# Logits of a sliding-window mixer: two bursts of 64 small matmuls in place of four of 32

## The chip, the cores and the metric

The kernel runs on one core of a Trainium2 chip. The metric is the device time of one execution, in microseconds. Three runs of the kernel before gave 169.6, 169.63 and 169.82 us; the median is 169.63.

A core has five engines, each with an instruction stream of its own that runs in order: TensorE (PE, with PEld for its weight loads), VectorE (DVE), ScalarE (ACT), GpSimd (POOL) and SyncE (SP). Here SP issues nearly all transfers from memory, ScalarE issues the small ones that spread the attention weights, and GpSimd does a few fills at the start. Engines wait for one another through semaphores.

## The reference

x is 2048 x 512. Two mixers read it, and a gate blends them row by row:

- g = sigmoid(sum over d of x * gate_w), one number for each row.
- a: q, k, v = x @ wqkv in 32 heads of 16. Row s attends to the eight rows s, s-2, ..., s-14 of its own head (rows before 0 are masked). The logits are q.k / 4, a softmax runs over the eight, the weighted sum of v follows, then @ wo.
- b: layer norm of each row of x, then a token MLP over the 2048 rows: u = gelu(h^T @ w1 + b1) with 1792 hidden units, y = u @ w2 + b2, transposed back.
- out = g * a + (1 - g) * b.

## The kernel before, in words

**The main stream.** TensorE runs one long sequence of 128x128 by 512 matmuls, in four parts: the projections q, k, v (line 594, named pf_ and pj_), the first MLP product (line 790, ph2_ft_qt: hidden tile ft of 14, quarter qt of the 16 row tiles), the second MLP product (line 840, ph3) and the output projection (line 856, wo_i). A block is four such matmuls. ScalarE copies the results out of four PSUM banks: projections at lines 602 and 605, gelu (gel_ft) at 811, the MLP's result (t1_i) at 907.

**The logits.** Projection columns are permuted so that each of four values dl holds four of a head's sixteen elements. VectorE multiplies q by k shifted by 0, 2, 4, 6 rows (wh = 0) or 8 to 14 rows (wh = 1), for each dl: that is f_qkm, line 664, named qkm_wh_dl_c. For wh = 0 each product is made in two halves of the rows (128x4096), for wh = 1 whole (128x8192). The products lie in four buffers PBL: 0 and 1 in region PBUF, 2 and 3 in region ATX. TensorE then sums each product over the 16 elements with small matmuls against a 0/1 matrix RP (f_qkr, line 672), 32 output columns wide, four of them side by side in the array. Each of four PSUM banks (4 to 7) holds the logits of one shift; all four dl accumulate in it. Before the change a stretch ("burst") covers two values of dl and has 32 matmuls: dl 0 and 1 in one operation, dl 2 and 3 in four operations, one for each bank. So there are four bursts, two for each wh. ScalarE copies each finished bank into ATT (lev_wh_wl, line 706).

**The softmax.** VectorE masks the first rows (msk_wh, line 716), takes maxima (sm_ma, sm_mb: line 722, scratch MX in region OUTS), subtracts (736), sums, divides and scales (751, 755); ScalarE does the exponentials (741). The weights go to ATX by transfers on ScalarE's queue (d_atx_u_a), and VectorE forms the weighted sum of v in eight units (avm, ava, avb, avc: lines 775 to 780).

**Statistics and gates.** VectorE computes the layer norm's statistics of the 16 row tiles (ln1_t, line 549), finishes them eight at a time (ln2a to ln2d, then ln_rstd and ln_nmr, called lnr here), and ScalarE normalises x in place (ln3_t, line 573). t_b (line 515) transposes the biases. The gate's sums gz_t (line 648) read a second copy of x: tiles 0 to 11 from XA (region WQKV, loaded by d_xa) and 12 to 15 from XB (loaded by d_xb). In the kernel before XB lies in buffer 2's region.

**The end.** cmb_i (line 877) on VectorE combines wo_i's PSUM bank with t1_i; the last four tiles are done in halves (a, b). Each result is stored at once.

**What sets the order.** No instruction stream is written out by hand. Every operation is given an engine, an estimated duration and the names that it reads and writes (`A(engine, fn, duration, reads, writes, ...)`); a list planner (`_Sched._pass`) walks them through time and puts each at the earliest start on its engine, ties going to the longer remaining path. A burst has a high priority and a `delay` of 0.05 beside a 0.06 latency, so it goes to the first block boundary of the main stream after its planned readiness. The planned order is then fixed, and the chip runs it with semaphores whatever the true durations are. `chain([...])` adds orders by hand: the long one for VectorE (line 936), one for SP (line 945) and one for ScalarE (line 951).

```
A("pe", f_qkr(prs), 2.0, reads=rd, writes=LGA, name="qkr_%d_%d" % (wh, dl), prio=-100, delay=BURST_DELAY)
rt = max(rt, d.end + lat + s_.delay)
```

Of the kernel before, what the change touches and what calls it, by code (L numbers as in the profile page):

```python
# [5 lines left out]
BF16 = mybir.dt.bfloat16  # L6
# [3 lines left out]
AF = mybir.ActivationFunctionType  # L10
# [3 lines left out]
D = 512  # L14
NH = 32
DH = 16
NW = 8
# [6 lines left out]
HC = 256  # L24
NEG = -1.0e9
NOELIDE = False
BURST_DELAY = 0.05
# [306 lines left out]
def bass_gated_mix__sliding_local_dilated__mixer_token_mlp__prompt_kernel(nc, A_x, A_wqkv, A_wo, B_x, B_w1, B_b1, B_w2, B_b2, gate_w, out, dbg=None):  # L334
    with contextlib.ExitStack() as es:
        block = es.enter_context(nc.Block())
        view, pview, off, total = _views(nc, es)
        ps = es.enter_context(nc.psum_tensor("ps", [128, 8, 512], FP32))
        esem = {e: es.enter_context(nc.semaphore("sem_" + e)) for e in ("pool", "act", "dve", "pe")}
        sch = _Sched()  # L340

        x2d = A_x[0]
        xv = x2d.rearrange("(t p) d -> p t d", p=128)
# [23 lines left out]
        ATX = view("ATX", BF16, [(NW * HC, 8), (HC, NW), (1, HC)])  # L367
        ATT = view("ATT", BF16, [(NW * HC, 2), (HC, NW), (1, HC)])
# [47 lines left out]
        A = sch.add  # L416
# [12 lines left out]
        def mk_dma(dst, src):  # L429
            return lambda e: e.dma_start(dst, src)  # L430
# [59 lines left out]
        def ld_w1(j):  # L490
# [4 lines left out]
            if j < 4:  # L495
# [8 lines left out]
                       writes=["wo"], deps=throttle(), after=prev_dma(), name="d_wo")  # L504
# [4 lines left out]
        for i_, (v_, n_) in enumerate(((B_b1, NFT), (B_b2, NST))):  # L509
            vr = v_.rearrange("(t q j) -> q t j", q=4, j=32)  # L510
            for q_ in range(4):
                sch.dma("sp", mk_dma(psub(BR, 32 * q_, n_, 32 * i_, [(1, 32)]), vr[q_]), n_ * 64, ds_b, reads=["br"],
                        writes=["br_%d_%d" % (i_, q_)], deps=throttle(), after=prev_dma(), name="d_b_%d_%d" % (i_, q_), issue=0.45)
        d_w1.append(ld_w1(3))
        A("dve", lambda e: e.transpose(out=BT, in_=BR), 0.2, reads=["br_%d_%d" % (i_, q_) for i_ in range(2) for q_ in range(4)],
          writes=["btc"], name="t_b")
# [29 lines left out]
        for hf in range(2):  # L546
            t0 = 8 * hf
            for t in range(t0, t0 + 8):
                A("dve", (lambda t_: (lambda e: e.bn_stats(out=ST6[:, t_, :], in_=X[:, t_, :])))(t), 0.59,  # L549
                  reads=["x%d" % t], writes=["st6_%d" % t], name="ln1_%d" % t, prio=0)  # L550
# [13 lines left out]
              reads=["zc%d" % hf], writes=["sd%d" % hf], name="ln_sqrt%d" % hf, prio=0)  # L564
            A("dve", (lambda t0_: (lambda e: e.reciprocal(out=cols(RSTD, t0_, 8), in_=cols(SD, t0_, 8))))(t0), 0.25,
              reads=["sd%d" % hf], writes=["rstd%d" % hf], name="ln_rstd%d" % hf, prio=0)
# [43 lines left out]
        for (b0, d0, d1, s0, s1) in ((0, 0, 1, 0, 512), (0, 1, 2, 0, 512), (0, 2, 3, 0, 512), (0, 3, 4, 0, 512), (4, 0, 2, 0, 512), (4, 2, 4, 0, 512)):  # L610
            for b in range(b0, b0 + 4):
                tn, dl = first[b]
# [21 lines left out]

        GWB = view("XT", BF16, [(1, D)], extra=NFT * D)
        XA = view("WQKV", BF16, [(D, 12), (1, D)])
        XB = view("ATX", BF16, [(D, 4), (1, D)], extra=3 * NW * HC)
        ds_xb = sch.dsem("xb")
        sch.dma("sp", mk_dma(XB, xv[:, 12:16, :]), 4 * 128 * D * 2, ds_xb, writes=["xb"], name="d_xb")
        ds_gw = sch.dsem("gw")  # L640
        gsrc = bass.AP(gate_w.tensor, gate_w.offset, [[0, 128], [1, D]])
        sch.dma("sp", mk_dma(GWB, gsrc), 128 * D * 2, ds_gw, writes=["gwb"], deps=[last_main[0]], name="d_gw")
# [3 lines left out]
        for t in range(NST):  # L646
            src = XA[:, t, :] if t < 12 else XB[:, t - 12, :]
            A("dve", (lambda s_, t_: (lambda e: e.scalar_tensor_tensor(out=s_, in0=s_, scalar=1.0, in1=GWB, op0=ALU.mult, op1=ALU.mult,  # L648
                                                                       accum_out=col(GZ, t_))))(src, t),
              0.6, reads=["xa" if t < 12 else "xb", "gwb"], writes=["gz%d" % t], name="gz_%d" % t)  # L650
        A("act", lambda e: e.activation(out=TH, in_=GZ, func=AF.Tanh, scale=0.5), 0.25, reads=["gz%d" % t for t in range(NST)],
          writes=["th"], name="g_tanh", prio=0)
        A("dve", lambda e: e.tensor_scalar(out=G, in0=TH, scalar1=0.5, scalar2=0.5, op0=ALU.mult, op1=ALU.add), 0.15,
# [12 lines left out]
        def f_qkr(pairs, wls=(0, 1, 2, 3)):  # L666
            def fn(e):
                ins = None
                for wl in wls:
                    for (dl, buf) in pairs:  # L670
                        for c in range(4):
                            ins = e.matmul(ps[32 * c:32 * c + 32, 4 + wl, :], lhsT=RP, rhs=PBL[buf][:, wl, c * 512:(c + 1) * 512],  # L672
                                           start=(dl == 0), stop=(dl == 3), tile_position=(0, 32 * c))
                return ins
            return fn

        def pbn(buf):
            return ["pb%d_0" % buf, "pb%d_1" % buf] if buf < 3 else ["lb0", "lb1"]

        LGA = ["lg%d_%d" % (b_, h) for b_ in range(4, 8) for h in range(2)]  # L680
        pb_readers = []
        k_all = ["k5_%d_%d" % (dl, sb) for dl in range(4) for sb in range(4)] + ["k5pad"]
        for wh in range(2):
            if wh == 0:
                pieces = [(dl, 2 * h, 2) for h in range(2) for dl in range(4)]
                bufs = [0, 1, 3, 2]
            else:
                pieces = [(dl, 0, 4) for dl in range(4)]
                bufs = [0, 1, 3, 0]
            for (dl, c0, nc_) in pieces:  # L690
                buf = bufs[dl]
                wr = pbn(buf) if nc_ == 4 else [pbn(buf)[c0 // 2]]
                A("dve", f_qkm(wh, dl, buf, c0, nc_), 4.4 if nc_ == 4 else 2.28,
                  reads=["q5_%d_%d" % (dl, sb) for sb in range(c0, c0 + nc_)] +
                        ["k5_%d_%d" % (dl, sb) for sb in range(max(c0 - 1, 0), c0 + nc_)] + ["k5pad"],
                  writes=wr, name="qkm_%d_%d_%d" % (wh, dl, c0), prio=0)
                if c0 + nc_ == 4 and dl % 2 == 1:
                    prs = [(dl - 1, bufs[dl - 1]), (dl, bufs[dl])]
                    rd = sum([pbn(b_) for _, b_ in prs], []) + ["rp"]
                    if dl == 1:  # L700
                        A("pe", f_qkr(prs), 2.0, reads=rd, writes=LGA, name="qkr_%d_%d" % (wh, dl), prio=-100, delay=BURST_DELAY)
                    else:
                        for wl in range(4):
                            qop = A("pe", f_qkr(prs, (wl,)), 0.5, reads=rd, writes=["lg%d_0" % (4 + wl), "lg%d_1" % (4 + wl)],
                                    name="qkr_%d_%d_%d" % (wh, dl, wl), prio=-100 + wl, delay=BURST_DELAY)
                            A("act", (lambda wh_, wl_: (lambda e: e.activation(out=ATT[:, :, 4 * wh_ + wl_, :], in_=ps[:, 4 + wl_, :].rearrange("p (h c) -> p h c", h=2), func=AF.Copy)))(wh, wl),
                              0.55, reads=["lg%d_0" % (4 + wl), "lg%d_1" % (4 + wl)], writes=["lw%d" % (4 * wh + wl)],
                              name="lev_%d_%d" % (wh, wl), prio=0)
                        pb_readers.append(qop)
            def f_msk(wh_):  # L710
                def fn(e):
                    res = []
                    for w in range(4 * wh_, 4 * wh_ + 4):
                        if w == 0:
                            continue
                        res.append(e.memset(psub(ATT, 0, 32, w * HC, [(1, 2 * w)]), NEG))
                    return res
                return fn
            A("dve", f_msk(wh), 0.3, writes=["lw%d" % w for w in range(4 * wh, 4 * wh + 4)], name="msk_%d" % wh, prio=0)
# [41 lines left out]
        for u in range(8):  # L761
            c, hf = u // 2, u % 2
# [57 lines left out]
        def ld_w2(j2):  # L820
            ds = sch.dsem("w2_%d" % j2)
            al = []
            dp = []
            if j2 < 2:
                dp = [byq["qkr_1_1"]]
            elif j2 == 2:
                al = ["wqkv%d_%d" % (tn, dt) for tn in range(3) for dt in range(4)] + ["gz%d" % t for t in range(12)]
            return sch.dma("sp", mk_dma(W2S[j2 % 3], w2v[:, :, 256 * j2:256 * j2 + 256]), F * 256 * 2, ds,
                           writes=["w2s%d" % (j2 % 3)] + al, deps=dp, name="d_w2_%d" % j2)
# [90 lines left out]
        def chain(names):  # L920
            for a_, b_ in zip(names, names[1:]):
                byname[b_].order.add(byname[a_])

        def ln1(*ts):
            return ["ln1_%d" % t for t in ts]

        def ln2(hf):
            return ["ln2%s%d" % (c_, hf) for c_ in "abcd"]

        def gz(*ts):  # L930
            return ["gz_%d" % t for t in ts]

        def lnr(hf):
            return ["ln_rstd%d" % hf, "ln_nmr%d" % hf]

        chain(["rp"] + ln1(0, 1, 2, 3) + ["qkm_0_0_0", "qkm_0_1_0"] + ln1(4, 5, 6, 7) + ln2(0)
              + ["qkm_0_2_0"] + lnr(0) + ["qkm_0_3_0", "qkm_0_0_2"] + ln1(8, 9) + ["qkm_0_1_2"] + ln1(10, 11, 12) + ["qkm_0_2_2"] + ln1(13, 14)
              + ["qkm_0_3_2", "qkm_1_0_0"] + ln1(15) + ln2(1) + ["t_b", "qkm_1_1_0"] + lnr(1)
              + ["qkm_1_2_0", "msk_0", "sm_ma0", "sm_mb0", "qkm_1_3_0"] + gz(12, 13, 14, 15, 0, 1) + [
                 "msk_1", "sm_ma1", "sm_mb1", "sm_m1", "sm_sub0", "sm_sub1"]  # L940
              + ["%s%d" % (n_, h_) for h_ in range(2) for n_ in ("sm_sa", "sm_sb", "sm_s1", "sm_rcp", "sm_nrm")] + gz(*range(2, 12))
              + ["%s_%d" % (n_, u) for k_ in range(4) for n_ in ("avm", "ava", "avb", "avc") for u in USEQ[2 * k_:2 * k_ + 2]] + ["cmb_%d" % i for i in range(HT0)] + ["cmb_%d%s" % (i, x_) for i in range(HT0, NST) for x_ in "ab"])
        byname["d_xb"].deps.update(byname["qkr_0_3_%d" % w] for w in range(4))
        byname["d_w1_6"].deps.add(byname["d_atx_2_3"])
        chain(["d_xb", "d_gw", "d_xa", "d_w2_0", "d_w2_1", "d_w1_4", "d_w1_5", "d_w1_6", "d_w2_2"])
        def atn(u):
            return ["d_atx_%d_%d" % (u, a_) for a_ in range(4)]

# [99 lines left out]
```

## Time and profile before

| | us |
|---|---|
| median of three runs | 169.63 |
| the profiled execution, its own time | 169.63 |
| span of the profiled execution | 167.8 |
| TensorE busy | 162.4 |
| VectorE busy | 150.7 |
| ScalarE busy | 75.0 |

The granted TensorE clock is full speed in every slice. "Busy" counts overlapped instructions once; the matmuls are pipelined, so their own durations (379 ns) are longer than the distance between two of them. The page's part 4 follows back, from the last instruction, what released each step. The timelines quoted below give, for each row, its start and its length in us from the span's start, the engine, line, operation, operands with shapes, the number of instructions merged into the row, and in brackets the idle time before it with what ended it.

### The profile page before, as it was taken

What the parts mean: (1) busy time and instruction counts of PE and PEld (TensorE: products, weight loads), DVE (VectorE), ACT (ScalarE), POOL (GpSimd) and SP (SyncE); (2) the same over time, 40 slices, a digit from 0 to 9 for tenths busy, and PEclk for the clock granted to TensorE, in tenths of its full rate; (3) what the DMA queues carried; (4) which work ended last, traced back from release to release, by engine and by line L of the source; (5) the groups of instructions that cost most, each with busy time, mean ns of one, the idle gap of its engine ahead of it and who ended that gap; (6) DMA issues with size and microseconds to landing.
All of it is one profiled execution on the core that took longest, in us unless ns stands there. A gap on an engine that the chain in (4) does not pass through costs nothing.

```text
span 167.8 us, 2139 instructions
## 1 busy us (share of the span) xinstructions
PE 162.4 (97%) x843; PEld 77.3 (46%) x858; DVE 150.7 (90%) x153; ACT 75.0 (45%) x115; POOL 0.7 (0%) x8
## 2 busy tenths in 40 slices
PE   7899999999999999999999999999999999999993
PEld 3455555544454444444444444444444444444462
DVE  0038999999999997799999999999999999999995
ACT  3087698898979819781131221131321312210000
POOL 1000000000000000000000000000000000000000
PEclk9999999999999999999999999999999999999999
DMA  6999999966304999555799906472573370000554
GB/s 145 286 244 273 280 325 292 298 190 174 129 0 115 356 294 287 152 145 145 177 276 328 288 9 151 103 207 83 147 219 116 103 223 0 0 0 0 184 181 139
DMA packets 47610, 29.64 MB, mean 177 GB/s; under 512 B 9841, under 2 KB 46449, under 8 KB 47601
## 3 DMA queue, kind: packets, MB, share of 16 engines
q1 hardware_dynamic: 45776, 25.11, 54.2%
q10 hardware_dynamic: 1824, 4.39, 9.4%
q8 instruction: 7, 0.11, 0.3%
q14 instruction: 3, 0.02, 0.0%
HBM read 21.11 MB, written 2.10 MB: 138 GB/s over the span
## 4 chain that ended last, share of the span: by engine, by line
PE 93%; DMA 3%; DVE 2%; issue 1%
PE ps L840 29%; PE ps L790 29%; PE ps L594 25%; PE ps L856 6%; PE ps L672 4%; DMA arena<-in_A_x_dram 3%; DVE arena L877 2%
## 5 line engine op out<-in xcount | busy, mean ns | idle before, releaser
L790 PE MATMUL ps<-arena 128*128 128x512 bf16 x219 | 48.2, 379 | 0.5 <-issue 0.3
L840 PE MATMUL ps<-arena 128*128 128x512 bf16 x220 | 48.5, 379 | 0.2
L594 PE MATMUL ps<-arena 128*128 128x512 bf16 x188 | 41.4, 379 | 1.1 <-DMA arena<-in_A_x_dram 0.7
L664 DVE TENSOR_TENSOR arena<-arena 128x4096 bf16<-128x4096 bf16 (+1 forms) x12 | 35.7, 2992 | 0.8 <-ACT arena L605 0.8
L775 DVE TENSOR_TENSOR arena<-arena 128x8192 bf16<-128x8192 bf16 x8 | 35.0, 4418 | 0.0
L790 PEld LDWEIGHTS ps<-arena 128*128 128x128 bf16 x224 | 21.7, 98 | 26.8 <-issue 0.8
L840 PEld LDWEIGHTS ps<-arena 128*128 128x128 bf16 x224 | 21.9, 98 | 26.4
L594 PEld LDWEIGHTS ps<-arena 128*128 128x128 bf16 x192 | 21.5, 113 | 21.0 <-issue 1.1
L907 ACT ACTIVATE arena<-ps,arena 128x512 bf16<-128x512 f32 x16 | 12.5, 778 | 39.4 <-PE ps L840 35.6
L778 DVE TENSOR_TENSOR arena<-arena 128x4096 bf16<-128x4096 bf16 (+1 forms) x16 | 27.0, 1752 | 0.0
L605 ACT ACTIVATE arena<-ps 128x512 bf16<-128x512 f32 x32 | 18.6, 597 | 5.3 <-PE ps L594 5.1
L811 ACT ACTIVATE arena<-ps,arena 128x512 bf16<-128x512 f32 x14 | 9.6, 689 | 23.7 <-PE ps L790 20.8
L549 DVE BATCH_NORM_STATS2 arena<-arena 128x6 f32<-128x512 bf16 x16 | 10.2, 682 | 9.8 <-DMA arena<-in_A_x_dram 9.8
L856 PE MATMUL ps<-arena 128*128 128x512 bf16 (+1 forms) x78 | 14.1, 335 | 0.1
L602 ACT ACTIVATE arena<-ps 128x512 bf16<-128x512 f32 x16 | 9.0, 597 | 7.4 <-PE ps L594 7.3
L573 ACT ACTIVATE arena<-arena 128x512 bf16<-128x512 bf16 x16 | 12.0, 803 | 0.0
L877 DVE SCALAR_TENSOR_TENSOR arena<-ps,arena 128x512 bf16<-128x512 f32 (+1 forms) x20 | 11.5, 638 | 0.4 <-PE ps L856 0.2
L856 PEld LDWEIGHTS ps<-arena 128*128 128x128 bf16 x80 | 7.8, 98 | 6.2
L648 DVE SCALAR_TENSOR_TENSOR arena<-arena 128x512 bf16<-128x512 bf16 x16 | 9.9, 686 | 0.0
L722 DVE TENSOR_TENSOR arena<-arena 128x512 bf16<-128x512 bf16 (+4 forms) x11 | 7.3, 667 | 1.2 <-ACT arena L741 0.8
L672 PE MATMUL ps<-arena 128*32 128x512 bf16 x128 | 7.6, 380 | 0.0
L780 DVE TENSOR_TENSOR arena<-arena 128x1024 bf16<-128x1024 bf16 x8 | 5.5, 689 | 0.1
(38 smaller groups left out, 37.6 us busy)
## 6 DMA issues: line engine op xcount, KB each, us to landing
arena<-in_B_w_dram SPq DMA_DIRECT2D x7, 1024.0 KB, 8.6
arena<-in_B_w_dram SPq DMA_DIRECT2D x8, 896.0 KB, 5.2
arena<-arena ACTq DMA_DIRECT2D x32, 128.0 KB, 2.7
arena<-in_A_x_dram SPq DMA_DIRECT2D x4, 512.0 KB, 4.7
out_dram<-arena SPq DMA_DIRECT2D x15, 128.0 KB, 1.7
arena<-in_A_x_dram SPq DMA_DIRECT2D x1, 1536.0 KB, 8.4
arena<-in_A_wqkv_dram SPq DMA_DIRECT2D x2, 256.0 KB, 3.9
arena<-in_A_x_dram SPq DMA_DIRECT2D x2, 256.0 KB, 3.9
```

What stands on the lines that cost most here:

```text
L573: A("act", (lambda t_: (lambda e: e.activation(out=X[:, t_, :], in_=X[:, t_, :], func=AF.Identity, scale=col(RSTD, t_), bias=col(NMR, t_)) ...
L594: ins = e.matmul(ps[:, bank, s0:s1], lhsT=lhsT, rhs=XT[:, dt, sb * 512 + s0:sb * 512 + s1], start=(dt == 0 and s0 == 0), stop=(dt == 3))
L605: return lambda e: e.activation(out=dst, in_=ps[:, bank, :], func=AF.Copy)
L664: return lambda e: e.tensor_tensor(out=PBL[buf][:, :, 512 * c0:512 * (c0 + nc_)], in0=in0, in1=in1, op=ALU.mult)
L672: ins = e.matmul(ps[32 * c:32 * c + 32, 4 + wl, :], lhsT=RP, rhs=PBL[buf][:, wl, c * 512:(c + 1) * 512], start=(dl == 0), stop=(dl == 3), ...
L775: A("dve", (lambda o_, i0, i1: (lambda e: e.tensor_tensor(out=o_, in0=i0, in1=i1, op=ALU.mult)))(pv, in0, in1), 4.4, reads=v_res + ["atx_% ...
L778: A("dve", (lambda pv_, n__: (lambda e: e.tensor_tensor(out=pv_[:, 0:n__], in0=pv_[:, 0:n__], in1=pv_[:, n__:2 * n__], op=ALU.add)))(pv, n ...
L790: ins = e.matmul(ps[:, bank, :], lhsT=W1W[:, slot, st, 128 * e_:128 * e_ + 128], rhs=X[:, st, :], start=(st == 0), stop=(st == NST - 1))
L840: ins = e.matmul(ps[:, bank, :], lhsT=W2S[slot][:, ft, 128 * e_:128 * e_ + 128], rhs=UT[:, ft, :], start=(ft == 0), stop=(ft == NFT - 1))
L856: ins = e.matmul(ps[:, bank, 0:c1 - c0], lhsT=OT[:, t, 128 * i:128 * i + 128], rhs=WO[:, t, c0:c1], start=(t == 0), stop=(t == 3))
L877: A("dve", (lambda i_, b_, c0_, c1_: (lambda e: e.scalar_tensor_tensor(out=T1[:, i_, c0_:c1_], in0=ps[:, b_, 0:c1_ - c0_], scalar=col(G, i ...
L907: A("act", (lambda i_, bank_: (lambda e: e.activation(out=T1[:, i_, :], in_=ps[:, bank_, :], func=AF.Identity, scale=col(OMG, i_), bias=co ...
```

## The change

- A burst covers all four dl: 64 matmuls, in four operations of 16, one for each PSUM bank, charged 0.92 each by the planner. There are two bursts, one for each wh, each ready when all its products are.
- For wh = 1 the four products take four different buffers (0, 1, 3, 2), where dl = 3 used buffer 0 a second time.
- XB moves from buffer 2's region to OUTS, which the maxima use as scratch: the gates 12 to 15 are declared as writers there, and they now stand ahead of msk_0, sm_ma0 and sm_mb0 on VectorE. d_xb no longer waits for the first half's logits.
- In VectorE's order ln1_10 to ln1_15 with ln2 stand behind the last product of wh = 0, not among them; lnr(1) stands a product earlier; msk_0 with its maxima stands behind qkm_1_3.
- On SP d_xb goes behind d_w1_3, and d_w1_4 goes ahead of d_w2_0 and d_w2_1. These two load into buffer 1's region and now wait for the second burst.

The core of the diff:

```diff
-        XB = view("ATX", BF16, [(D, 4), (1, D)], extra=3 * NW * HC)
+        XB = view("OUTS", BF16, [(D, 4), (1, D)])
...
-                bufs = [0, 1, 3, 0]
+                bufs = [0, 1, 3, 2]
...
-                if c0 + nc_ == 4 and dl % 2 == 1:
-                    prs = [(dl - 1, bufs[dl - 1]), (dl, bufs[dl])]
-                    rd = sum([pbn(b_) for _, b_ in prs], []) + ["rp"]
-                    if dl == 1:
-                        A("pe", f_qkr(prs), 2.0, reads=rd, writes=LGA, name="qkr_%d_%d" % (wh, dl), prio=-100, delay=BURST_DELAY)
-                    else:
-                        for wl in range(4):
-                            qop = A("pe", f_qkr(prs, (wl,)), 0.5, reads=rd, writes=["lg%d_0" % (4 + wl), "lg%d_1" % (4 + wl)],
-                                    name="qkr_%d_%d_%d" % (wh, dl, wl), prio=-100 + wl, delay=BURST_DELAY)
...
+            rd = sum([pbn(b_) for b_ in bufs], []) + PBX[wh] + ["rp"]
+            for wl in range(4):
+                qop = A("pe", f_qkr(list(enumerate(bufs)), (wl,)), 0.92, reads=rd, writes=["lg%d_0" % (4 + wl), "lg%d_1" % (4 + wl)],
+                        name="qkr_%d_%d" % (wh, wl), prio=-100 + wl, delay=BURST_DELAY)
...
-                dp = [byq["qkr_1_1"]]
+                dp = [byq["qkr_1_3"]]
...
-              + ["qkm_0_2_0"] + lnr(0) + ["qkm_0_3_0", "qkm_0_0_2"] + ln1(8, 9) + ["qkm_0_1_2"] + ln1(10, 11, 12) + ["qkm_0_2_2"] + ln1(13, 14)
-              + ["qkm_0_3_2", "qkm_1_0_0"] + ln1(15) + ln2(1) + ["t_b", "qkm_1_1_0"] + lnr(1)
-              + ["qkm_1_2_0", "msk_0", "sm_ma0", "sm_mb0", "qkm_1_3_0"] + gz(12, 13, 14, 15, 0, 1) + [
+              + ["qkm_0_2_0"] + lnr(0) + ["qkm_0_3_0", "qkm_0_0_2"] + ln1(8, 9) + ["qkm_0_1_2", "qkm_0_2_2", "qkm_0_3_2"] + ln1(*range(10, 16)) + ln2(1)
+              + ["t_b", "qkm_1_0_0"] + lnr(1) + ["qkm_1_1_0"]
+              + ["qkm_1_2_0", "qkm_1_3_0"] + gz(12, 13, 14, 15) + ["msk_0", "sm_ma0", "sm_mb0"] + gz(0, 1) + [
...
-        byname["d_xb"].deps.update(byname["qkr_0_3_%d" % w] for w in range(4))
...
-        chain(["d_xb", "d_gw", "d_xa", "d_w2_0", "d_w2_1", "d_w1_4", "d_w1_5", "d_w1_6", "d_w2_2"])
+        chain(["d_w1_3", "d_xb", "d_gw", "d_xa", "d_w1_4", "d_w2_0", "d_w2_1", "d_w1_5", "d_w1_6", "d_w2_2"])
```

More of the change, by code (lines that the diff above doesn't have):

```diff
@@ L636, in bass_gated_mix__sliding_local_dilated__mixer_token_mlp__prompt_kernel @@
         XA = view("WQKV", BF16, [(D, 12), (1, D)])
-        XB = view("ATX", BF16, [(D, 4), (1, D)], extra=3 * NW * HC)
+        XB = view("OUTS", BF16, [(D, 4), (1, D)])
         ds_xb = sch.dsem("xb")
-        sch.dma("sp", mk_dma(XB, xv[:, 12:16, :]), 4 * 128 * D * 2, ds_xb, writes=["xb"], name="d_xb")
+        sch.dma("sp", mk_dma(XB, xv[:, 12:16, :]), 4 * 128 * D * 2, ds_xb, writes=["xb"] + ["outs%d" % k for k in range(4)], name="d_xb")
         ds_gw = sch.dsem("gw")
@@ L649, in bass_gated_mix__sliding_local_dilated__mixer_token_mlp__prompt_kernel @@
                                                                        accum_out=col(GZ, t_))))(src, t),
-              0.6, reads=["xa" if t < 12 else "xb", "gwb"], writes=["gz%d" % t], name="gz_%d" % t)
+              0.6, reads=["gwb"] + (["xa"] if t < 12 else ["xb"]), writes=["gz%d" % t] + ([] if t < 12 else ["outs%d" % (t - 12)]), name="gz_%d" % t)
         A("act", lambda e: e.activation(out=TH, in_=GZ, func=AF.Tanh, scale=0.5), 0.25, reads=["gz%d" % t for t in range(NST)],
@@ L681, in bass_gated_mix__sliding_local_dilated__mixer_token_mlp__prompt_kernel @@
         pb_readers = []
+        PBX = [[], []]
         k_all = ["k5_%d_%d" % (dl, sb) for dl in range(4) for sb in range(4)] + ["k5pad"]
@@ L696, in bass_gated_mix__sliding_local_dilated__mixer_token_mlp__prompt_kernel @@
                   writes=wr, name="qkm_%d_%d_%d" % (wh, dl, c0), prio=0)
-                if c0 + nc_ == 4 and dl % 2 == 1:
-                    prs = [(dl - 1, bufs[dl - 1]), (dl, bufs[dl])]
-                    rd = sum([pbn(b_) for _, b_ in prs], []) + ["rp"]
-                    if dl == 1:
-                        A("pe", f_qkr(prs), 2.0, reads=rd, writes=LGA, name="qkr_%d_%d" % (wh, dl), prio=-100, delay=BURST_DELAY)
-                    else:
-                        for wl in range(4):
-                            qop = A("pe", f_qkr(prs, (wl,)), 0.5, reads=rd, writes=["lg%d_0" % (4 + wl), "lg%d_1" % (4 + wl)],
-                                    name="qkr_%d_%d_%d" % (wh, dl, wl), prio=-100 + wl, delay=BURST_DELAY)
[L706 to L709, printed above, removed]
+            rd = sum([pbn(b_) for b_ in bufs], []) + PBX[wh] + ["rp"]
+            for wl in range(4):
+                qop = A("pe", f_qkr(list(enumerate(bufs)), (wl,)), 0.92, reads=rd, writes=["lg%d_0" % (4 + wl), "lg%d_1" % (4 + wl)],
+                        name="qkr_%d_%d" % (wh, wl), prio=-100 + wl, delay=BURST_DELAY)
+                A("act", (lambda wh_, wl_: (lambda e: e.activation(out=ATT[:, :, 4 * wh_ + wl_, :], in_=ps[:, 4 + wl_, :].rearrange("p (h c) -> p h c", h=2), func=AF.Copy)))(wh, wl),
+                  0.55, reads=["lg%d_0" % (4 + wl), "lg%d_1" % (4 + wl)], writes=["lw%d" % (4 * wh + wl)],
+                  name="lev_%d_%d" % (wh, wl), prio=0)
+            pb_readers.append(qop)
             def f_msk(wh_):
```

## The prediction

> **What bounds the kernel now.** First the page: its busy line and its chain.
>
> ```profile
> PE 162.4 (97%) x843; PEld 77.3 (46%) x858; DVE 150.7 (90%) x153; ACT 75.0 (45%) x115; POOL 0.7 (0%) x8
> PE 93%; DMA 3%; DVE 2%; issue 1%
> PE ps L840 29%; PE ps L790 29%; PE ps L594 25%; PE ps L856 6%; PE ps L672 4%; DMA arena<-in_A_x_dram 3%; DVE arena L877 2%
> ```
>
> TensorE is busy for 97% of the span and carries 93% of the chain, so what it saves counts, if VectorE, 90% busy, can follow. Next, the TensorE timeline (start, us, engine, line, operation, count): L672 is the logits' bursts, and between them lies the main stream.
>
> ```profile
> 33.81 1.91 PE L672 MATMUL ps<-arena 128*32 128x512 bf16 x32
> 35.89 5.13 PE L594 MATMUL ps<-arena 128*128 128x512 bf16 x23 [0.17 <-issue]
> 40.95 1.91 PE L672 MATMUL ps<-arena 128*32 128x512 bf16 x32
> 43.03 7.72 PE L594 MATMUL ps<-arena 128*128 128x512 bf16 x35 [0.17 <-issue]
> 50.59 1.03 PE L790 MATMUL ps<-arena 128*128 128x512 bf16 x4
> 51.55 1.91 PE L672 MATMUL ps<-arena 128*32 128x512 bf16 x32
> 53.62 8.58 PE L790 MATMUL ps<-arena 128*128 128x512 bf16 x39 [0.16 <-issue]
> 62.13 1.91 PE L672 MATMUL ps<-arena 128*32 128x512 bf16 x32
> 64.19 38.80 PE L790 MATMUL ps<-arena 128*128 128x512 bf16 x176 [0.16 <-issue]
> 102.83 45.49 PE L840 MATMUL ps<-arena 128*128 128x512 bf16 x206
> ```
>
> No waits on VectorE stand here: each burst finds its products ready. Three narrow windows of the timeline show a burst inside (the first, second and last group).
>
> ```profile
> 33.81 0.40 PE L672 MATMUL ps<-arena 128*32 128x512 bf16 x4
> 34.03 0.39 PE L672 MATMUL ps<-arena 128*32 128x512 bf16 x4
> ...
> 35.33 0.39 PE L672 MATMUL ps<-arena 128*32 128x512 bf16 x4
> ```
>
> From burst to burst are 7.14, 10.60 and 10.58 us, and by the code six, ten and ten blocks of four main matmuls lie between (a record is missing after each burst, so I count in the code). Four blocks more thus take 3.46 and 3.44 us: 0.863 a block on the mean, 0.216 a matmul. A burst takes the rest, 7.14 - 6 x 0.863 = 1.96, and 1.97 and 1.95 in the other intervals. Inside it four small matmuls start together, and the eight groups are (35.33 - 33.81) / 7 = 0.217 apart. Eight groups are 1.73; so each burst costs 0.23 at its borders, whatever it computes.
>
> Last, the end. VectorE's timeline of the combining line L877, and five of its instructions from narrow windows:
>
> ```profile
> 153.85 3.38 DVE L877 SCALAR_TENSOR_TENSOR arena<-ps,arena 128x512 bf16<-128x512 f32 x5
> 157.42 8.30 DVE L877 SCALAR_TENSOR_TENSOR arena<-ps,arena 128x512 bf16<-128x512 f32 x15 [0.19 <-PE ps L856]
> ```
> ```profile
> 161.74 0.75 DVE L877 SCALAR_TENSOR_TENSOR arena<-ps,arena 128x512 bf16<-128x512 f32 x1
> 162.41 0.48 DVE L877 SCALAR_TENSOR_TENSOR arena<-ps,arena 128x256 bf16<-128x256 f32 x1
> ...
> 164.36 0.48 DVE L877 SCALAR_TENSOR_TENSOR arena<-ps,arena 128x256 bf16<-128x256 f32 x1
> 164.79 0.48 DVE L877 SCALAR_TENSOR_TENSOR arena<-ps,arena 128x256 bf16<-128x256 f32 x1
> 165.23 0.49 DVE L877 SCALAR_TENSOR_TENSOR arena<-ps,arena 128x256 bf16<-128x256 f32 x1
> ```
>
> Undisturbed, whole tiles are (3.38 - 0.74) / 4 = 0.66 apart and half tiles (164.36 - 162.41) / 5 = 0.39. Alone VectorE would end at 153.85 + 12 x 0.66 + 7 x 0.39 + 0.49 = 164.99. It ends at 165.72: the eighth projection holds it to 161.74, and the last halves come 0.43 apart, as TensorE delivers them. So TensorE sets the end, and VectorE has 0.73 us of slack, no more. That makes two lines to follow.
>
> **The TensorE line.** The same 128 small matmuls run, in two bursts. One of 64 is 1.96 + 8 x 0.217 = 3.69; two are 7.38, and four were 7.84. Gain 0.46. Bounds: nothing, if the 0.23 belongs to the groups and grows with the burst; 0.80, if the two "issue" gaps of 0.17 came on top of it, though the intervals already hold them. I take 0.46, since it comes from start times alone and three intervals agree. [...]
>
> **Where the bursts land.** The planner fixes the order by its charges (literals in the code, used here for the order alone). In both kernels it has statistics tile ln1_9 done at 30.45 and the block pj_v0_0 at 33.52. VectorE then: three half products 3 x 2.28 = 6.84, to 37.29; burst 1 is ready 0.11 later, at 37.40; the running block ends at 33.52 + 5 x 0.866 = 37.85. So burst 1 follows pj_v1_1 and ends at 37.85 + 4 x 0.92 = 41.53. VectorE continues: six statistics 3.54, ln2 0.72, t_b 0.20, to 41.75; qkm_1_0 4.40; lnr 0.45; three products 13.20, to 59.80; burst 2 is ready at 59.91. TensorE: ten blocks to 50.19, then ph2 blocks of 0.864; the eleventh ends at 59.69, the twelfth at 60.56. Burst 2 comes after the twelfth, ph2_2_3, by 0.22.
>
> On the chip: burst 1 begins at 33.81 + 5 x 0.863 = 38.13 and its last group finishes at 38.13 + 15 x 0.217 + 0.39 = 41.77. Burst 2 begins at 33.81 + 27 x 0.863 + 3.69 = 60.81.
>
> **The VectorE line.** No instruction of its own is added or removed.
>
> ```profile
> 30.30 2.27 DVE L664 TENSOR_TENSOR arena<-arena 128x4096 bf16<-128x4096 bf16 x1
> 32.49 1.87 DVE L549 BATCH_NORM_STATS2 arena<-arena 128x6 f32<-128x512 bf16 x3
> 34.28 2.27 DVE L664 TENSOR_TENSOR arena<-arena 128x4096 bf16<-128x4096 bf16 x1
> ...
> 44.20 0.69 DVE L549 BATCH_NORM_STATS2 arena<-arena 128x6 f32<-128x512 bf16 x1
> ...
> 45.66 4.38 DVE L664 TENSOR_TENSOR arena<-arena 128x8192 bf16<-128x8192 bf16 x1
> ...
> 50.28 4.42 DVE L664 TENSOR_TENSOR arena<-arena 128x8192 bf16<-128x8192 bf16 x1
> 54.64 0.08 DVE L716 MEMSET arena<- 32x2 bf16 x3
> ...
> 55.84 4.42 DVE L664 TENSOR_TENSOR arena<-arena 128x8192 bf16<-128x8192 bf16 x1
> 60.17 0.69 DVE L648 SCALAR_TENSOR_TENSOR arena<-arena 128x512 bf16<-128x512 bf16 x1
> ...
> 64.91 0.12 DVE L716 MEMSET arena<- 32x8 bf16 x4 [0.99 <-ACT arena L706]
> ```
>
> Start to start, a half product is 2.19, a statistics tile 0.60, a product 4.33, and ln1_15 with ln2 and t_b 1.46. Three halves from 30.30 end at 36.87; five tiles and the 1.46 end at 41.31. There lies a new wait: qkm_1_0 overwrites buffer 0, which all of burst 1 reads, so it starts at about 41.85, 0.54 late. Then 4.62 (45.66 to 50.28, with lnr) and three products of 4.33 reach 59.46, 1.35 before burst 2: TensorE is not held. Six gates, 60.17 to 63.92 (the wait's 0.99 before 64.91), are 3.75; msk_0 with its two maxima, 54.64 to 55.84, 1.20. Moved behind qkm_1_3, these keep VectorE busy to 64.41.
>
> Then msk_1 waits for the last logits copy. Two of ScalarE's copies, from narrow windows (first and last of four):
>
> ```profile
> 62.79 0.60 ACT L706 ACTIVATE arena<-ps 128x512 bf16<-128x512 f32 x1 [2.46 <-PE ps L672]
> ...
> 64.24 0.62 ACT L706 ACTIVATE arena<-ps 128x512 bf16<-128x512 f32 x1
> ```
>
> Bank one had two groups, 0.43 us, and its copy began 0.66 after the burst's start, so 0.23 after its matmuls. Copies run 0.48 apart. A bank now takes four groups, 0.87, so copies keep up and the last begins at 60.81 + 16 x 0.217 + 0.23 = 64.51, ends at 65.11, and msk_1 starts at 65.15: 0.24 later than before. The 0.54 at burst 1 vanishes in this wait, which shrinks from 0.99 to 0.74. Behind msk_1 the chain to the combine is rigid, its exponential waiting on VectorE's own subtraction. ScalarE's gel_1 queues behind the copies; its bank is next wanted eight blocks after the burst, 6.9 us. Bounds of the 0.24: -0.50, no wait left (64.41 for 64.91); +1.10, one block later.
>
> **Moves at no cost.** The statistics before ln3 come earlier, so its tiles are earlier too, ahead of ph2's second half. The two queue moves need their covers:
>
> ```profile
> 42.91 0.39 SPq L430 DMA_DIRECT2D arena<-in_A_x_dram  x1
> ```
> ```profile
> arena<-in_B_w_dram SPq DMA_DIRECT2D x8, 896.0 KB, 5.2
> arena<-in_A_x_dram SPq DMA_DIRECT2D x1, 1536.0 KB, 8.4
> ```
>
> d_xb, at 42.91, now goes right behind d_w1_3, into a region nobody uses; its gates run near 59.5. d_gw and d_xa wait for the last v block as before; d_xa lands 8.4 after about 51, before gz_0 near 63.1. d_w2_0 and d_w2_1 now wait for burst 2, near 64.5, 11 us later than its old release; they take 5.2 and are first read at 102.83, so 30 us cover them. Behind them on SP stands d_w1_5, whose slot is free only four blocks after burst 2; d_w1_4, moved ahead, waits for nothing new. If that cover failed, L790 would stop for the slab.
>
> **Sum.** The TensorE line ends at 165.72 - 0.46 = 165.26, the VectorE line at 164.99 + 0.24 = 165.23. The later counts: -0.46. The profiled execution took 169.63 with a span of 167.8, and the runs' median is the same 169.63: 169.63 - 0.46 = 169.17. The lines meet within 0.03, so little more is to be had and delay on VectorE shows at once.
>
> **Rivals.** A: VectorE takes over. If msk_1 is late by 0.45 instead of 0.24 (copies slower behind the longer burst), it ends at 165.44, time 169.35. For it: 0.23 of latency rests on one copy; against: ScalarE is idle 2.46 us before it.
>
> B: slower. Burst 2 falls one block later; msk_1 moves by 0.86, VectorE ends at 166.09, 0.37 above 165.72: 170.00. It decides as soon as msk_1 is over 0.73 late. For it: my walk is by hand, and order is quantised in blocks of 0.863; against: readiness would have to be 0.65 later. (One block earlier leaves 169.17: TensorE still ends last.)
>
> C: the change does not do what it says: the border cost grows with the burst. Each burst of 64 then takes 3.92, TensorE saves nothing, and msk_1 comes 0.24 + 2 x 0.23 = 0.70 late, just inside VectorE's slack: 169.63. Against: the groups inside a burst run evenly, so the cost is not in them.
>
> **How the numbers follow.** Forecast 0.50, A 0.16, C 0.12, B 0.17, and 0.05 for another wait on TensorE near 170.2. Faster by over 0.2% (0.34 us, about what a measurement can tell from no change) is the forecast, 0.50; A and C are no change, 0.28; B and the rest slower, 0.22. The forecast's own range is 169.05 to 169.29. The range given, 169.0 to 170.0, takes in A, C and half of B.
>
> **What would show it.** L672 in two rows of 64, from 38.1 and 60.8, each costing the main stream 3.7; a wait of some 0.5 on PE before the first 128x8192 product; a wait of some 0.7 at msk_1, near 65.15; L877 with hardly any idle time, its first at 154.1 and its last starting near 164.8. Wrong if burst 2 starts at 59.9 or 61.7, if TensorE waits on VectorE or ScalarE, or if the last halves come 0.39 apart from a first combine past 154.4.

## The result, and the profile after

The changed kernel takes 169.31 us (median of 22 runs, 169.03 to 170.04); the kernel before, run beside it, 169.81 (22 runs, 169.47 to 170.53). The ratio is 0.9973, with a 95% interval of 0.9963 to 0.9983. That is 0.27% less, the size that was forecast (169.17 for 169.63 is 0.27%), although both medians lie somewhat higher than the numbers the sum was made against; the last section shows where executions of one kernel part. 169.31 is 0.02 above the forecast's own narrow range and inside the range given. The interval stands for 0.29 to 0.63 us: the times show a gain of about this size, and whether it is 0.46 has to be read from the profiles.

The page of the changed kernel, its busy line and its chain:

```profile
PE 163.2 (98%) x858; PEld 77.6 (46%) x858; DVE 150.6 (90%) x153; ACT 74.7 (45%) x115; POOL 0.7 (0%) x8
DVE 57%; PE 35%; DMA 3%; ACT 2%; issue 1%
PE ps L594 25%; DVE arena L771 21%; DVE arena L774 16%; DVE arena L873 7%; PE ps L786 6%; PE ps L672 4%; DVE arena L718 4%; DVE arena L648 4%; DMA arena<-in_A_x_dram 3%; DVE arena L747 2%; DVE arena L776 2%; DVE arena L751 1%; ACT arena L737 1%; DVE arena L732 1%; ACT arena L702 0%
```

TensorE is as busy as before, but the chain now leaves it at the second burst and runs through VectorE for the rest: the two lines have met. (Lines behind the change are four lower than in the kernel before: the MLP is L786 and L836, the combine L873, the mask L712, the copy L702.) The TensorE timeline:

```profile
5.17 32.97 PE L594 MATMUL ps<-arena 128*128 128x512 bf16 x152 [0.61 <-DMA arena<-in_A_x_dram]
38.06 3.64 PE L672 MATMUL ps<-arena 128*32 128x512 bf16 x64
41.63 8.82 PE L594 MATMUL ps<-arena 128*128 128x512 bf16 x40
50.29 10.52 PE L786 MATMUL ps<-arena 128*128 128x512 bf16 x48
60.75 3.64 PE L672 MATMUL ps<-arena 128*32 128x512 bf16 x64
64.32 38.16 PE L786 MATMUL ps<-arena 128*128 128x512 bf16 x176
```

Two bursts of 64, at 38.06 and 60.75. From one to the other are 22.69 us and 22 blocks (40 + 48 matmuls): 22.69 - 22 x 0.863 = 3.70 for a burst. The second MLP product (L836) begins at 102.31, which is 64.25 behind burst 1; before the change it began at 102.83, 64.70 behind the same place in the main stream (33.81 + 5 x 0.863 = 38.13). TensorE's line is 0.45 shorter. VectorE's two waits, and its end:

```profile
41.76 4.43 DVE L664 TENSOR_TENSOR arena<-arena 128x8192 bf16<-128x8192 bf16 x1 [0.42 <-PE ps L672]
...
59.42 0.68 DVE L648 SCALAR_TENSOR_TENSOR arena<-arena 128x512 bf16<-128x512 bf16 x1
...
65.09 0.13 DVE L712 MEMSET arena<- 32x8 bf16 x4 [0.69 <-ACT arena L702]
...
154.03 11.17 DVE L873 SCALAR_TENSOR_TENSOR arena<-ps,arena 128x512 bf16<-128x512 f32 x20
```

The combine runs its 20 instructions without a recorded wait and ends at 165.20. Three of its last instructions, from narrow windows:

```profile
163.90 0.47 DVE L873 SCALAR_TENSOR_TENSOR arena<-ps,arena 128x256 bf16<-128x256 f32 x1
164.29 0.48 DVE L873 SCALAR_TENSOR_TENSOR arena<-ps,arena 128x256 bf16<-128x256 f32 x1
164.72 0.48 DVE L873 SCALAR_TENSOR_TENSOR arena<-ps,arena 128x256 bf16<-128x256 f32 x1
```

Up to the last but one they come 0.39 apart, VectorE's own pace; the last comes 0.43 later, TensorE's pace. So both engines reach the end within 0.04 us of one another.

### The profile page after: what moved, and what is told of

The parts are those of the page before. It is cut to its first block, busy times and chain, and to the rows that moved or that the text cites. A ratio compares the mean times of both kernels' runs of the same rounds, so it can differ in the third digit from the quotient of the medians.

```text
span 167.3 us, 2153 instructions
## 1 busy us (share of the span) xinstructions
PE 163.2 (98%) x858; PEld 77.6 (46%) x858; DVE 150.6 (90%) x153; ACT 74.7 (45%) x115; POOL 0.7 (0%) x8
## 4 chain that ended last, share of the span: by engine, by line
DVE 57%; PE 35%; DMA 3%; ACT 2%; issue 1%
PE ps L594 25%; DVE arena L771 21%; DVE arena L774 16%; DVE arena L873 7%; PE ps L786 6%; PE ps L672 4%; DVE arena L718 4%; DVE arena L648 4%; DMA arena<-in_A_x_dram 3%; DVE arena L747 2%; DVE arena L776 2%; DVE arena L751 1%; ACT arena L737 1%; DVE arena L732 1%; ACT arena L702 0%
## 5 line engine op out<-in xcount | busy, mean ns | idle before, releaser
L786 PE MATMUL ps<-arena 128*128 128x512 bf16 x224 | 48.7, 379 | 0.0
L836 PE MATMUL ps<-arena 128*128 128x512 bf16 x224 | 48.7, 379 | 0.0
L786 PEld LDWEIGHTS ps<-arena 128*128 128x128 bf16 x224 | 21.8, 98 | 26.6 <-ACT arena L702 0.4
L836 PEld LDWEIGHTS ps<-arena 128*128 128x128 bf16 x224 | 21.9, 98 | 26.5
L605 ACT ACTIVATE arena<-ps 128x512 bf16<-128x512 f32 x32 | 18.6, 596 | 4.7 <-PE ps L594 4.7
L807 ACT ACTIVATE arena<-ps,arena 128x512 bf16<-128x512 f32 x14 | 9.6, 687 | 22.0 <-PE ps L786 15.7
L602 ACT ACTIVATE arena<-ps 128x512 bf16<-128x512 f32 x16 | 9.0, 596 | 7.4 <-PE ps L594 7.3
L873 DVE SCALAR_TENSOR_TENSOR arena<-ps,arena 128x512 bf16<-128x512 f32 (+1 forms) x20 | 11.2, 634 | 0.0
L702 ACT ACTIVATE arena<-ps 128x512 bf16<-128x512 f32 x8 | 4.7, 593 | 4.6 <-PE ps L672 4.6
```

The costliest lines, as they stand in the source:

```text
L605: return lambda e: e.activation(out=dst, in_=ps[:, bank, :], func=AF.Copy)
L786: ins = e.matmul(ps[:, bank, :], lhsT=W1W[:, slot, st, 128 * e_:128 * e_ + 128], rhs=X[:, st, :], start=(st == 0), stop=(st == NST - 1))
L836: ins = e.matmul(ps[:, bank, :], lhsT=W2S[slot][:, ft, 128 * e_:128 * e_ + 128], rhs=UT[:, ft, :], start=(ft == 0), stop=(ft == NFT - 1))
L873: A("dve", (lambda i_, b_, c0_, c1_: (lambda e: e.scalar_tensor_tensor(out=T1[:, i_, c0_:c1_], in0=ps[:, b_, 0:c1_ - c0_], scalar=col(G, i ...
```

## The experiments

Profiled executions differ by up to 0.7 us ahead of the first burst, where TensorE's stream is the same in all these kernels (last section). Profiles are therefore compared from the start of burst 1 in the changed kernel. In the kernel before, that point lies five blocks behind its first burst, 33.81 + 5 x 0.863 = 38.13; where burst 1 itself moved, I use its old place. Each row's positions come from one profiled execution.

| kernel | ratio to before (95%) | burst 1 | mask after it | first combine after it | end after it |
|---|---|---|---|---|---|
| before | 1 | 38.13 | 26.78 | 115.72 | 127.59 |
| changed | 0.9973 (0.9963 to 0.9983) | 38.06 | 27.03 | 115.97 | 127.14 |
| three bursts | 0.9985 (0.9971 to 0.9999) | 38.77 | 26.27 | 115.22 | 127.35 |
| changed, VectorE less | 0.9970 (0.9957 to 0.9983) | 38.08 | 27.02 | 115.50 | 127.14 |
| changed, TensorE less | 0.9961 (0.9947 to 0.9975) | 38.52 | 27.02 | 115.96 | 127.08 |
| changed, both less | 0.9952 (0.9935 to 0.9969) | 38.59 | 27.02 | 115.50 | 126.62 |
| before, VectorE less | 0.9998 (0.9981 to 1.0014) | 38.16 | 26.79 | 115.27 | 127.59 |
| before, TensorE less | 0.9961 (0.9933 to 0.9989) | 38.29 | 26.78 | 115.73 | 126.85 |
| burst 2 a block later | 1.0021 (1.0005 to 1.0037) | 38.31 | 27.89 | 116.84 | 127.96 |
| burst 2 a block earlier | 0.9977 (0.9962 to 0.9991) | 38.14 | 26.27 | 115.21 | 127.13 |
| statistics among the products | 1.0131 (1.0107 to 1.0155) | 38.04 | 29.61 | 118.56 | 129.68 |

The mask is msk_1; the end is that of the last combine. The theory is the prediction's: a burst costs TensorE a fixed time at its borders, and the end is the later of two lines, which now are level. The rival is that TensorE's borders are worth nothing and VectorE's new order brought the gain.

**What a border costs.** Work is added to the changed kernel in its second MLP product, where nothing else changes: eight groups of four small matmuls at eight places, or in one, or eight full-size matmuls at the eight places.

```diff
+            if 2 <= i < 10:      # or: if i == 5, with 8 groups
+                last_main[0] = A("pe", f_probe(1), 0.45, reads=["wo", "rp"], writes=["lg7_0", "lg7_1"],
+                                 after=[last_main[0]], name="probe_%d" % i, prio=0)
```

> The changed kernel with work added: one group of four small matmuls (0.217 us) behind each of the blocks ph3b_2 to ph3b_9, eight groups at eight places. Theory (a burst costs 0.23 us at its borders, however long it is): TensorE's main stream is longer by 8 x (0.217 + 0.23) = 3.58 us, and so is the time, about 172.8. Rival (the 0.23 belongs to the groups, 0.245 a group): longer by 1.96, time about 171.2.

> The changed kernel with the same eight groups added in one burst behind ph3b_5. Theory and rival agree on it: 8 x 0.217 + 0.23 = 1.96 us longer on TensorE, time about 171.2. It is the measure for the eight apart.

> The changed kernel with one full-size matmul (128x128 by 512) added at each of the same eight places. Theory (the border is that of the tiling, not of an added operation, another bank or other weights): 8 x 0.216 = 1.73 us longer on TensorE. Rival (any stray operation between two blocks costs a border): 8 x (0.216 + 0.23) = 3.57.

TensorE's timeline of the first, the stage's beginning, three of the probes (L899), and the output projection that follows the stage:

```profile
103.03 9.23 PE L836 MATMUL ps<-arena 128*128 128x512 bf16 x42
112.18 0.40 PE L899 MATMUL ps<-arena 128*32 128x512 bf16 x4
112.52 3.19 PE L836 MATMUL ps<-arena 128*128 128x512 bf16 x14
115.64 0.40 PE L899 MATMUL ps<-arena 128*32 128x512 bf16 x4
...
136.38 0.40 PE L899 MATMUL ps<-arena 128*32 128x512 bf16 x4
136.71 15.28 PE L836 MATMUL ps<-arena 128*128 128x512 bf16 x70
151.83 3.62 PE L852 MATMUL ps<-arena 128*128 128x512 bf16 x16
```

Of the second (eight groups together):

```profile
102.70 18.29 PE L836 MATMUL ps<-arena 128*128 128x512 bf16 x84
120.93 1.91 PE L899 MATMUL ps<-arena 128*32 128x512 bf16 x32
122.77 27.37 PE L836 MATMUL ps<-arena 128*128 128x512 bf16 x126
149.97 3.62 PE L852 MATMUL ps<-arena 128*128 128x512 bf16 x16
```

Of the third (full-size matmuls), and of the changed kernel itself:

```profile
102.63 9.23 PE L836 MATMUL ps<-arena 128*128 128x512 bf16 x42
...
149.68 3.62 PE L852 MATMUL ps<-arena 128*128 128x512 bf16 x16
```
```profile
102.31 45.49 PE L836 MATMUL ps<-arena 128*128 128x512 bf16 x210
147.64 3.62 PE L852 MATMUL ps<-arena 128*128 128x512 bf16 x16
```

From the stage's beginning to the output projection are 48.80, 47.27, 47.05 and 45.33 us: 3.47, 1.94 and 1.72 more than in the changed kernel. The full-size matmuls cost their 0.215 and nothing else, so an added operation, another bank or other full-size weights are not what costs. Seven borders more cost 3.47 - 1.94 = 1.53, 0.22 each; one burst of eight groups costs 1.94 - 8 x 0.217 = 0.20 beside its groups. The cost is that of a burst and not of its groups. From burst 1 on, the last combine ends 3.48, 1.94 and 1.71 later than in the changed kernel, so the whole kernel pays it. The times, 173.23, 171.38 and 171.05 us from a single run of each, are 4.18, 2.33 and 2.00 above the changed kernel's profiled run (169.05); the rest is that burst 1 itself began 0.71, 0.39 and 0.32 later in them. That is why the first lies 0.4 above the 172.8 that was expected.

What happens at a border, the weight loads (PEld) show. First the load of one of the eight groups and of the main stream behind it, then the load and the start of a full-size matmul (L898):

```profile
112.18 0.10 PEld L899 LDWEIGHTS ps<-arena 128*32 128x32 bf16 x4 [0.42 <-issue]
112.51 2.70 PEld L836 LDWEIGHTS ps<-arena 128*128 128x128 bf16 x14 [0.23 <-issue]
```
```profile
111.48 0.10 PEld L898 LDWEIGHTS ps<-arena 128*128 128x128 bf16 x1
111.69 0.38 PE L898 MATMUL ps<-arena 128*128 128x512 bf16 x1
```

The full-size matmul's weights are loaded 0.21 ahead of it, beside the matmul before it. On both sides of the small group the load begins only with its own matmul (112.18 and 112.51, for matmuls at 112.18 and 112.52); the small group's four loads last 0.10 together, a load of the main stream takes 98 ns on the mean (L836 in the changed kernel's page). So at each of these borders the load is not covered by the work before it. Whether this late load is what takes the 0.22, no run here shows.

**One burst split again.** The second half's logits in two bursts of 32:

```diff
+            if wh == 1:
+                A("pe", f_qkr(prs[:2]), 2.0, reads=..., writes=LGA, name="qkr_1a", prio=-100, delay=BURST_DELAY)
+                prs = prs[2:]
```

> One part undone: the second half's logits (wh = 1) in two bursts of 32 again, all else as changed. Theory: one border more, TensorE's line 0.23 later than in the changed kernel; the last burst is short and ready early, so VectorE does not wait at the mask (start near 64.35 instead of 65.09) and its line is 0.7 earlier; TensorE ends last, time +0.2 over the changed kernel, ratio to the kernel before about 0.9985. Rival (the gain is VectorE's, from its new order and shorter wait): time 0.5 to 0.7 below the changed kernel, ratio about 0.994.

VectorE's timeline of it, the mask and the combine:

```profile
65.04 0.12 DVE L717 MEMSET arena<- 32x8 bf16 x4
...
153.99 3.38 DVE L878 SCALAR_TENSOR_TENSOR arena<-ps,arena 128x512 bf16<-128x512 f32 x5
157.83 8.29 DVE L878 SCALAR_TENSOR_TENSOR arena<-ps,arena 128x512 bf16<-128x512 f32 x15 [0.46 <-PE ps L857]
```

The mask has no wait left and starts 26.27 after burst 1, 0.76 earlier than in the changed kernel, and all that is given back at the combine, where VectorE waits 0.46 for TensorE in the record (more hides in slower spacings behind it: from first start to last end the combines take 12.13, against 11.12 at VectorE's own pace). The end is 127.35, 0.21 later than in the changed kernel, the price of one border; the ratio is 0.9985 as expected. The rival, under which the earlier VectorE should have gained, falls.

**Which line ends last.** VectorE or TensorE or both are given less to do, in both kernels. What is left out: most of one gate sum (its first 64 columns stay), and one block of the first MLP product.

```diff
+            nc_ = 64 if t in VCUT else D          # VCUT = (11,)
+            src = XA[:, t, 0:nc_] if t < 12 else XB[:, t - 12, 0:nc_]
...
+            emit_ph2(ft, (2, 3) if ft < 3 else (0, 1, 2) if ft == NFT - 1 else (0, 1, 2, 3))
```

> The changed kernel with gate sum 11 taken over 64 of its 512 columns, which leaves out most of that tile's sum: VectorE has 0.3 to 0.55 us less to do late in its line, TensorE the same. Theory (the two lines now end level, within some 0.05): time lower by 0 to 0.1 only, the last combines paced by TensorE. Rival (VectorE alone sets the end now, with room under it): lower by all of the 0.3 to 0.55.

> The changed kernel without the last block of the first MLP product's last tile (four matmuls, 0.863 us, left out of the sum): TensorE shorter by 0.86, VectorE the same. Theory (level lines): time lower by 0 to 0.1 only, no TensorE wait in the combines. Rival (TensorE still bounds the kernel with VectorE well ahead): lower by 0.5 or more.

> The changed kernel with both cuts (most of gate sum 11 and the MLP block left out). Theory (level lines, each held by the other): time lower by 0.3 to 0.55, the whole VectorE cut, since TensorE is now 0.86 ahead. Rival (either line alone bounds): the same as whichever single cut moved the time.

> The kernel before with gate sum 11 taken over 64 of its 512 columns (most of that tile's sum left out). Theory (VectorE has 0.73 us of slack there, TensorE sets the end): no change, within 0.05 us. Rival (VectorE is the bound before the change too): lower by 0.3 to 0.55.

> The kernel before without the last block of the first MLP product's last tile (four matmuls, 0.863 us, left out). Theory: TensorE 0.86 shorter, but VectorE's slack is 0.73, so the time is lower by 0.70 to 0.76, ratio about 0.9957, and VectorE runs its combines without waiting. Rival (TensorE bounds by more than that): the whole 0.86. Second rival (VectorE bounds): 0.

The combine rows of VectorE's timelines, in that order:

```profile
153.58 11.64 DVE L875 SCALAR_TENSOR_TENSOR arena<-ps,arena 128x512 bf16<-128x512 f32 x20
```
```profile
154.48 11.12 DVE L873 SCALAR_TENSOR_TENSOR arena<-ps,arena 128x512 bf16<-128x512 f32 x20
```
```profile
154.09 11.12 DVE L875 SCALAR_TENSOR_TENSOR arena<-ps,arena 128x512 bf16<-128x512 f32 x20
```
```profile
153.43 3.38 DVE L879 SCALAR_TENSOR_TENSOR arena<-ps,arena 128x512 bf16<-128x512 f32 x5
157.46 8.29 DVE L879 SCALAR_TENSOR_TENSOR arena<-ps,arena 128x512 bf16<-128x512 f32 x15 [0.66 <-PE ps L858]
```
```profile
154.02 11.12 DVE L877 SCALAR_TENSOR_TENSOR arena<-ps,arena 128x512 bf16<-128x512 f32 x20
```

The VectorE cut is worth 0.47 (first combine 115.97 to 115.50). In the changed kernel it moves the end by 0.00: the combine takes 11.64 instead of 11.17, because TensorE now paces it. The TensorE cut of 0.86 moves the end by 0.06: VectorE's own pace, 11.12. Both together move it by 0.52, which is 0.47 + 0.06 within rounding. In the kernel before, the VectorE cut moves the end by 0.00 and only lengthens the wait (0.66 in the record for 0.19), and the TensorE cut moves it by 0.74, not by its 0.86: the slack that the prediction read off the combine's spacing was 0.73. By the ratios alone the four forms of the changed kernel (0.9952 to 0.9973) are not clearly told apart, since their intervals overlap; the verdict rests on the profiles.

**Where burst 2 is put.** Only the planner's delay of the second burst is changed:

```diff
-  delay=BURST_DELAY
+  delay=BURST_DELAY if wh == 0 else 0.80      # the other kernel: -0.18
```

> The changed kernel with the planner's delay of the second burst raised, so that it comes one block of 0.863 us later (13 blocks, not 12); nothing else moves. Theory: the mask starts 0.86 later, near 65.95, TensorE's line is unchanged, VectorE's sets the end: time +0.83 to +0.86 over the changed kernel, ratio to the kernel before about 1.002. Rival (the wait is hidden behind other work of VectorE): no change.

> The changed kernel with the planner's delay of the second burst lowered, so that it comes one block earlier (11 blocks). Theory: burst 2 near 59.9 still finds its products ready; the wait of 0.69 at the mask goes (start near 64.35), VectorE's line is 0.7 earlier, but TensorE's line stays: time lower than the changed kernel by 0 to 0.1, and the last combines wait for TensorE again. Rival (VectorE alone bounds the changed kernel): lower by 0.6 to 0.7, ratio to the kernel before about 0.993.

VectorE's timeline of the later one, then of the earlier one:

```profile
66.20 0.12 DVE L712 MEMSET arena<- 32x8 bf16 x4 [1.56 <-ACT arena L702]
...
155.15 11.12 DVE L873 SCALAR_TENSOR_TENSOR arena<-ps,arena 128x512 bf16<-128x512 f32 x20
```
```profile
64.41 0.12 DVE L712 MEMSET arena<- 32x8 bf16 x4
...
153.35 3.38 DVE L873 SCALAR_TENSOR_TENSOR arena<-ps,arena 128x512 bf16<-128x512 f32 x5
156.98 8.29 DVE L873 SCALAR_TENSOR_TENSOR arena<-ps,arena 128x512 bf16<-128x512 f32 x15 [0.25 <-PE ps L852]
```

One block later costs 0.86 at the mask and 0.82 at the end, and the kernel is then slower than before the change (1.0021, 1.0005 to 1.0037). One block earlier brings 0.76 at the mask and 0.01 at the end. So the change stands next to a step: from one block to the next it turns from gain to loss.

**VectorE's order undone.** The statistics of tiles 10 to 15 stand among the products again:

```diff
-  ["qkm_0_1_2", "qkm_0_2_2", "qkm_0_3_2"] + ln1(*range(10, 16)) + ln2(1)
+  ["qkm_0_1_2"] + ln1(10, 11, 12) + ["qkm_0_2_2"] + ln1(13, 14) + ["qkm_0_3_2"] + ln1(15) + ln2(1)
```

> One part undone: statistics of tiles 10 to 15 stand among the products of wh = 0, as before the change. Theory (with long bursts VectorE's place at burst 1 sets everything behind it): burst 1 three blocks later, near 40.65; the wait before the first product of wh = 1 grows from 0.42 to about 3.0; burst 2 three blocks later, near 63.3; end and time +2.6 over the changed kernel, about 171.9, some 1.3% over the kernel before. Rival (the merged bursts gain whatever VectorE's order is, as the wait at the mask absorbs it): within 0.3 of the changed kernel.

Its VectorE wait at burst 1, and a row of its TensorE timeline:

```profile
44.32 4.42 DVE L664 TENSOR_TENSOR arena<-arena 128x8192 bf16<-128x8192 bf16 x1 [3.01 <-PE ps L672]
```
```profile
76.48 27.80 PE L786 MATMUL ps<-arena 128*128 128x512 bf16 x128 [1.66 <-ACT arena L807]
```

The wait is 3.01, the mask 2.58 later, the end 2.54 later, 1.3% slower than before the change. Not foreseen was TensorE's 1.66 us wait for gelu (L807): in the changed kernel's ScalarE timeline the next gelus (73.18) come behind the exponentials (68.15), which wait for VectorE's subtraction, and here the subtraction had moved back with the mask (L732, to 69.46 from 66.89). That the gelus were late for this reason is worked out from these starts. It cost nothing here because VectorE was later still: its 20 combines take 11.12, its own pace, without a wait. Without the new order of the statistics the merged bursts lose far more than they bring.

## Why the prediction was right, point by point

- **The TensorE line.** "One of 64 is 1.96 + 8 x 0.217 = 3.69": measured 3.70. The bound of no gain, if the cost belonged to the groups (rival C), is excluded by the groups set apart. The probe's border is 0.20 to 0.22, the one read from the intervals 0.23. The full-size matmuls, which keep the main stream's 128x128 form, cost 0.215 each and nothing extra. The weight load that begins only with its own matmul at a border would fit the cost, but the border's cost is shown and its mechanism is not.
- **Where the bursts land.** Predicted 38.13 and 60.81, measured 38.06 and 60.75, with burst 2 behind twelve blocks. All positions lie some 0.06 early because this execution's stream began that much earlier.
- **The new wait at burst 1.** Predicted 0.54, recorded 0.42. The record counts from the end of t_b (41.34); in the kernel before, the next instruction started 0.16 behind t_b's start, which here gives 41.26 and a wait of 0.50. It cost nothing, as the next wait absorbed it.
- **The mask.** Predicted 65.15 and a wait of 0.74; measured 65.09 and 0.69. The latency taken from one copy held: the last copy began 3.69 behind burst 2, for 3.70. So the mask came 0.25 later than before the change (27.03 for 26.78), not the 0.45 of rival A.
- **The sum.** Predicted ends 165.26 for TensorE and 165.23 for VectorE; measured 165.20, with the last half tile 0.04 behind VectorE's pace. The end is 0.45 earlier from burst 1 on (127.59 to 127.14), for 0.46.
- **Moves at no cost.** The queue moves show no wait in the changed kernel's chain. They were not tried by themselves.
- **Rival B** was real in its price and its sign: the block-later kernel shows it. It did not occur because the hand-walked order was right. The 0.22 was its margin to the block before; to the block behind, which is rival B, it was 0.65. Both margins held in the planner: 0.23 less delay brought burst 2 a block earlier, 0.75 more a block later.

## What to carry to other kernels

Before merging or splitting a burst, read its border cost from start-to-start intervals with the work between them counted in the code, not from "issue" rows or single durations. Then look at the spacing of the last instructions on each engine: whoever comes at its own pace is the bound, and the difference to the other's pace, summed, is the slack; a gain on one engine is worth at most that slack. And where a planner or a list puts work at block boundaries, work out the margin to the next boundary, because one block decided here between 0.3% faster and 0.2% slower.

## What the runs showed of the hardware that was not expected

The changed kernel's runs spread over 1 us (169.03 to 170.04). In the profiles of these kernels up to 0.7 us of such a difference arises ahead of burst 1, most of it in the first microseconds. TensorE's first projections in narrow windows, of the changed kernel and of the kernel with eight groups apart, whose program is the same up to there:

```profile
5.17 0.38 PE L594 MATMUL ps<-arena 128*128 128x512 bf16 x1 [0.61 <-DMA arena<-in_A_x_dram]
5.38 0.59 PE L594 MATMUL ps<-arena 128*128 128x512 bf16 x2
```
```profile
5.18 0.59 PE L594 MATMUL ps<-arena 128*128 128x512 bf16 x1
5.18 1.01 PE L594 MATMUL ps<-arena 128*128 128x512 bf16 x2
6.00 0.63 PE L594 MATMUL ps<-arena 128*128 128x512 bf16 x1
```

In the one a matmul lasts 0.38 and the next begins 0.21 later; in the other it lasts 0.59 to 0.63 and they begin about 0.4 apart until some time past 6 us. Burst 1 then starts at 38.06 or at 38.77, and the whole remaining execution is shifted. The other kernels lie between these or next to the early one (38.04 to 38.59). The ten warm-up matmuls (L526) ahead of the projections read a constant and no loaded data, and they show the same two paces, again in the changed kernel and in the one with eight groups apart:

```profile
0.84 3.72 PE L526 MATMUL ps<-const-bfloat16-1.0 128*128 128x512 bf16 x10 [0.84 <-PEq L1028]
```
```profile
0.84 4.21 PE L526 MATMUL ps<-const-bfloat16-1.0 128*128 128x512 bf16 x10 [0.84 <-PEq L1040]
```

In the one the faster pace sets in before the warm-up ends, in the other not: the last three matmuls of it, from 3.78 on, take 0.78 us in the one and 1.27 in the other. In the five profiles with a warm-up of 3.54 to 3.76, burst 1 has its place at 38.04 to 38.14, in the nine with 4.17 to 4.21 at 38.16 to 38.77. So in these profiles the spread comes mainly from the moment at which the pace doubles, and not from a load. The granted clock in the profile's windows says 1.00 for both, so that row does not show it. What sets the moment, no run here shows. One execution (three bursts) also waited 0.29 us for a load of x. Since this part is common to all kernels, differences of 0.2 us between them show in profiles measured from a common point, and in medians only with many runs.
